# A fused attention, soft-MoE and maxout kernel: another order between its second and third stage, filler transposes, and one load taken a step earlier

## Chip, cores and metric

The kernel runs on one core of a Trainium2 chip. The metric is the device time of one execution in microseconds (us). The engines are TensorE (PE; its weight loads are PEld), VectorE (DVE), ScalarE (ACT), GpSimd (POOL) and SyncE (SP), which issues almost all DMAs of this kernel, in the order of its queue.

## What is computed

Three stages follow each other; everything is float32 to the outside, and the last stage's weights come in as float64.

```python
# 1. attention in chunks of 64 tokens: q, k, v are [8 batches, 8 heads, 576, 64]
scores = scale * q_c @ k_c.T;  attn = softmax(scores);  x = attn @ v_c
x = x as [4608 tokens, 512]
# 2. soft mixture of 8 experts, 4 slots each (32 slots)
logits = x @ phi                                   # [4608, 32]
d = softmax(logits over the tokens);  slot_input = d.T @ x      # [32, 512]
for e in range(8): slot_out[e] = relu(slot_input[e] @ w1[e]) @ w2[e]   # 512 -> 1024 -> 512
c = softmax(logits over the slots);  y = c @ slot_out
# 3. maxout
out = max(y @ w1, y @ w2, y @ w3) @ w_out          # 512 -> 768 -> 512
```

The softmax over the tokens is the reason for the narrow place that the change is about: no slot input exists before the last token's logits do.

## The kernel before, in words

**Items.** The first stage is cut into 36 items (`NI`): an item is 256 tokens of four heads. A hand-written list, `ORDER` (line 63), names the steps of one turn; the loop at line 573 runs the list once for every i, and a step with an offset works on another item than i (`item(f, d)` gives i + d). So in turn i, PE transposes q and k of item i + 3 (`Tq`, `Tk`, line 239), multiplies q and k of item i (`S`, line 271), transposes the scores (`PT`, line 303) and multiplies with v (`PV`, line 319) of item i - 1, and transposes x (`XT`, line 354) of item i - 2. ACT copies the transposed q and k out of PSUM (`qe`, `ke`, line 252) and takes the exponentials. Every fourth turn has the logits of 512 tokens (`lg`, line 372) and their part of the slot sum (`slp`, line 428).

**Weights of the third stage.** They arrive as float64 and are turned into float32 piece by piece, one of 30 pieces in each turn: `LR` (line 559) issues the load of raw piece i in turn i into a pool of two buffers (`r64_p`, line 151); in turn i + 1 ACT makes a first conversion (`da`, line 495), and DVE finishes it in three steps (`d0`, `d1`, `d2`, lines 500 to 506). `da` stands ahead of `ke` in ACT's queue.

**Loads.** SP issues, in each turn and in the order of the list, the raw piece, quarters of the first experts' weights (line 139), and q, k (line 179) and v (line 203) of later items. q and k of item i + 5 are loaded in turn i and transposed in turn i + 2. In turns 1 to 4 the last 64 tokens of all batches are loaded as well (line 191).

**Between items and experts** (lines 588 to 682). The last items run out; the logits of each group, kept in `lsb` as [slots, tokens], are transposed to [tokens, slots] (`emit_lt`, line 447: one PE transpose and one ACT copy a group; 9 groups). The last logits give the last maximum (`emit_final_max`), the exponentials, their transpose (`eps`, line 414), a maximum for all slots (`mt`, `mb`), the last slot product (`slp`), its accumulation on DVE (`acc`, line 437), the slot input (`sip`, line 669, copied to `siT`) and the sum of weights (`tot`, line 677). Then the first expert's product can start (`hps`, line 689).

**Experts** (line 778 on). Their weights, 32 pieces of 1 MB, go through a ring of 19 buffers; the buffers beyond twelve open when pools of the first stage close, and pieces 20 to 32 wait for buffers that the experts release. Then follow the last weights (`wr`) and the third stage, where PE computes all through (lines 872 and 909).

Of the kernel before, what the change touches and what calls it, by code (L numbers as in the profile page):

```python
# [8 lines left out]
F32 = mybir.dt.float32  # L9
# [11 lines left out]
def kernel(  # L21
# [14 lines left out]
    nc = tc.nc  # L36
    B, H, S, D = q.shape
    NT, DM = out.shape
    E, _, F = w1.shape
# [7 lines left out]
    NG = NU // 2  # L47
# [100 lines left out]
    v_p = tc.alloc_tile_pool(name="vp", bufs=1, side="right")  # L148
    q_p = tc.alloc_tile_pool(name="qp", bufs=3, side="right")
    raw_p = tc.alloc_tile_pool(name="raw", bufs=2, side="right")  # L150
    r64_p = tc.alloc_tile_pool(name="r64", bufs=2, side="right")
    ps_t = p1.enter_context(tc.tile_pool(name="ps_t", bufs=4, space=PSUM))
    ps_q = ps_t
    ps_s = p1.enter_context(tc.tile_pool(name="ps_s", bufs=1, space=PSUM))
# [18 lines left out]
    def load_T(j, nm):  # L173
        if J8 <= j < J8 + 4:
            return
        src = q if nm == "qr" else k
        t = raw_p.tile([128, 2, 4, D], F32, tag=nm, name=nm)
        h0 = 2 * (j % 4)
        nc.sync.dma_start(
            out=t, in_=src[DUS[j // 4], h0:h0 + 2, 0:2 * UNIT, :].rearrange("m (p r) d -> p m r d", r=4)  # L180
        )
        raw[nm, j] = t
# [195 lines left out]
    def emit_lcopy(g):  # L378
        nc.vector.tensor_copy(out=lsb[:, g, :], in_=lgs.pop(g))
# [32 lines left out]
    def emit_eT(g):  # L412
        ps = ps_t.tile([128, 128], F32, tag="t", name="eps")
        nc.tensor.transpose(ps, e_sb[g], ident)
        eps[g] = ps
# [18 lines left out]
    def emit_slot_acc(g):  # L434
        ps, nm = slp.pop(g), al.pop(g)
        if g:
            nc.vector.scalar_tensor_tensor(
                out=acc, in0=acc, scalar=nm[:, 1:2], in1=ps, op0=ALU.mult, op1=ALU.add
            )
        else:  # L440
            nc.vector.tensor_copy(out=acc, in_=ps)
# [2 lines left out]
        emit_slot_mm(g)  # L444
        emit_slot_acc(g)

    def emit_lt(g):
        ps = ps_q.tile([128, 128], F32, tag="t", name="lt")
        nc.tensor.transpose(ps, lsb[:, g, :], ident)
        nc.scalar.copy(out=lsb[:, g, :], in_=ps)  # L450

# [36 lines left out]
    def load_raw(n):  # L488
        src, dst = dec[n]
        t = r64_p.tile([128, DW, 2], I32, tag="r64", name="r64")[:, 0:dst.shape[-1], :]  # L490
        nc.sync.dma_start(out=t, in_=src.bitcast(I32).rearrange("p (n t) -> p n t", t=2))
        dec_t[n] = t
# [19 lines left out]
    if True:  # L512
        make_identity(nc, ident)
        nc.vector.tensor_copy(out=identb, in_=ident)
        for j in range(2):
            load_T(j, "qr")
            load_T(j, "kr")
        load_v(0, nc.scalar)
        load_v(1, nc.scalar)
        for t in vt:  # L520
            nc.gpsimd.memset(t[:, :, 128:130], 1.0)
            nc.gpsimd.memset(t[:, :, 194:196], 1.0)
        load_raw(0)
        nc.sync.dma_start(out=phi_sb, in_=phi.rearrange("(k p) s -> p k s", p=128))
        for j in range(3):
            emit_T(j)
            if j < 2:
                emit_qevac(j)
                emit_kevac(j)
            load_T(j + 2, "qr")  # L530
            load_T(j + 2, "kr")
        nc.gpsimd.memset(ones1, 1.0)

        def at(i, d):
            g, r = divmod(i - d, 4)
            return g if r == 0 and 0 <= g < NG else None

        def item(f, d):
            return lambda i: f(i + d) if 0 <= i + d < NI else None

        def group(f, d):
            return lambda i: f(at(i, d)) if at(i, d) is not None else None

        def dstep(part):
            def f(i):
                n = i - 1
                if 0 <= n < len(dec):
                    if part < 0:
                        decode_a(dec_t[n], dec[n][1])
                    else:  # L550
                        decode_b(dec_t[n], dec[n][1], part)
            return f

        def lstep_c(i):
            if i > 4:
                load_quarter()

        STEPS = {
            "LR": lambda i: load_raw(i) if 0 < i < len(dec) else None,
            "LQ": item(lambda j: load_T(j, "qr"), 5), "LK": item(lambda j: load_T(j, "kr"), 5),  # L560
            "LV": item(load_v, 2), "LC": lstep_c, "LD": lambda i: lstep_c(i) if i % 2 else None,
            "LS": lambda i: load_S(i - 1) if 1 <= i <= 4 else None,
            "VS": item(emit_vswap, 0),
            "qe": item(emit_qevac, 2), "S": item(emit_S, 0), "PT": item(emit_PT, -1), "PTe": item(emit_PTe, -1),
            "da": dstep(-1), "ke": item(emit_kevac, 2), "ex": group(emit_exps, 7), "sm": group(emit_slot_mm, 9),
            "sa": group(emit_slot_acc, 9), "Tq": item(lambda i: emit_T(i, ("qr",)), 3), "mx": item(emit_max, 0),
            "sub": item(emit_sub, 0), "XT": item(emit_XT, -2), "XTe": item(emit_XTe, -2),
            "d0": dstep(0), "d1": dstep(1), "d2": dstep(2), "PV": item(emit_PV, -1), "rd": item(emit_rd, -1),
            "rec": item(emit_rec, -1), "nrm": item(emit_norm, -1), "eT": group(emit_eT, 8), "eTe": group(emit_eTe, 8),
            "Tk": item(lambda i: emit_T(i, ("kr",)), 3), "lg": group(emit_logits, 6), "lc": group(emit_lcopy, 6),  # L570
            "st": group(emit_stats, 6), "ss": group(emit_ssum, 7),
        }
        for i in range(NI):
            for name in ORDER.split():
                STEPS[name](i)
            if i == len(dec) + 1:
                r64_p.release()
                open_rings(1)
                nc.vector.tensor_reduce(
                    out=sel, in_=ident.rearrange("p (g s) -> p s g", g=4), axis=AX.X, op=ALU.max  # L580
                )
            if i == NI - 4:
                raw_p.release()
                open_rings(1)
        q_p.release()
        open_rings(1)

        last = NG - 1
        emit_PT(NI - 1)
        emit_PTe(NI - 1)  # L590
        emit_eT(last - 1)
        emit_eTe(last - 1)
        emit_XT(NI - 2)
        emit_XTe(NI - 2)
        emit_PV(NI - 1)
        v_p.release()
        w1_p.release()
        open_rings(2)
        emit_rd(NI - 1)
        emit_rec(NI - 1)  # L600
        emit_norm(NI - 1)
        emit_slot(last - 1)
        xb_p.release()
        open_rings(1)
        for g in range(4):
            emit_lt(g)
        emit_XT(NI - 1)
        emit_XTe(NI - 1)
        emit_logits(last)
        xt_p.release()  # L610
        open_rings(1)
        emit_lcopy(last)
        emit_final_max()
        emit_eT(last)
        emit_eTe(last)
        emit_max_bcast()
        for g in range(4, last):
            emit_lt(g)
        emit_slot_mm(last)
        nc.vector.tensor_scalar(out=dg, in0=sel, scalar1=wv[:, 0:1], scalar2=None, op0=ALU.mult)  # L620
        emit_ssum(last)
        nc.vector.tensor_tensor(out=wv[:, 1:2], in0=wv[:, 0:1], in1=ssum, op=ALU.mult)
        emit_slot_acc(last)

    p1.close()
    m_p = ctx.enter_context(tc.tile_pool(name="m_p", bufs=1, side="right", reuse_waits="tile"))
# [37 lines left out]
    if True:  # L664
        for t in hzb:
            nc.gpsimd.memset(t, 0.0)
        sip = ps2.tile([128, KM, NS], F32, tag="b", name="sip")
        for kk in range(KM):
            nc.tensor.matmul(
# [1 line left out]
            )  # L671
        siT = m_p.tile([128, KM, NS], F32, name="siT")
        nc.vector.tensor_copy(out=siT, in_=sip)
        for g in range(4):
            nc.vector.tensor_copy(out=same[:, g, :], in_=sel)
        tot = ps2.tile([128, 1], F32, tag="b", name="tot")
        nc.tensor.matmul(tot, lhsT=same.rearrange("p g s -> p (g s)"), rhs=wv[:, 1:2], start=True, stop=True)
        nc.vector.tensor_scalar(out=wv[:, 2:3], in0=tot, scalar1=EPS, scalar2=None, op0=ALU.add)
        nc.vector.reciprocal(out=wv[:, 2:3], in_=wv[:, 2:3])
        lt = ps2.tile([128, 128], F32, tag="b", name="lt")  # L680
        nc.tensor.transpose(lt, lsb[:, NG - 1, :], ident)
        nc.scalar.copy(out=lsb[:, NG - 1, :], in_=lt)

        def emit_w1(e):
            ps = ps2b.tile([128, 256], F32, tag="h", name="hps")
# [14 lines left out]
        def emit_ht(e, hs):  # L700
            pt = ps2.tile([128, 2, 4, NS], F32, tag="b", name="hpt")
            for b in range(2):
                nc.tensor.transpose(
                    pt[:, b].rearrange("p j s -> p (j s)"), hs[:, 128 * b:128 * b + 128], ident
                )
            hz = hzb[e % 2]
            if e >= 2:
                nc.vector.memset(hz[:, :, SPE * (e - 2):SPE * (e - 1)], 0.0)
            nc.vector.tensor_copy(
                out=hz[:, :, SPE * e:SPE * e + SPE].rearrange("p (j b) s -> p b j s", b=2),  # L710
                in_=pt[:, :, :, SPE * e:SPE * e + SPE],
            )
# [62 lines left out]
                    b = stacks.pop(0)  # L775
                    ready.append((b, emit_stack(b)))

        emit_ht(0, emit_w1(0))
        for e in range(E):
            if e == E - 2:  # L780
                emit_w2(e, 0)
# [281 lines left out]
```

## Time and profile before

| | us |
|---|---|
| median of 3 timed runs (lowest, highest) | 450.44 (447.75, 451.75) |
| the profiled execution's own time | 447.13 |
| its span, first to last instruction | 445.3 |
| PE busy | 405.9 (91%) |
| DVE, ACT, POOL busy | 260.4, 215.7, 157.3 |
| mean granted clock of PE, in shares of full speed | 0.973 |

The items take the span up to about 180 us, the stretch between items and experts goes to about 193.5 us, the experts end at about 236 us and the third stage fills the rest. The DMA engines' busy share is 0.8 and more until about 190 us, near zero for some us there, full again until about 238 us, and 0.2 or less in the third stage. In what follows, a clock of 1.00 is 2.4 GHz and one of 0.50 is 1.2 GHz, PE's two levels; a mean between them is a stretch that had both.

### The profile page before, as it was taken

What the parts mean: (1) busy time and instruction counts of PE and PEld (TensorE: products, weight loads), DVE (VectorE), ACT (ScalarE), POOL (GpSimd) and SP (SyncE); (2) the same over time, 40 slices, a digit from 0 to 9 for tenths busy, and PEclk for the clock granted to TensorE, in tenths of its full rate; (3) what the DMA queues carried; (4) which work ended last, traced back from release to release, by engine and by line L of the source; (5) the groups of instructions that cost most, each with busy time, mean ns of one, the idle gap of its engine ahead of it and who ended that gap; (6) DMA issues with size and microseconds to landing.
All of it is one profiled execution on the core that took longest, in us unless ns stands there. A gap on an engine that the chain in (4) does not pass through costs nothing.

```text
span 445.3 us, 13226 instructions
## 1 busy us (share of the span) xinstructions
PE 405.9 (91%) x5505; PEld 303.4 (68%) x5505; DVE 260.4 (58%) x581; ACT 215.7 (48%) x393; POOL 157.3 (35%) x261
## 2 busy tenths in 40 slices
PE   5888978999899898789989799999999999999996
PEld 4766666767677676343345677888888888888884
DVE  0748777889788677426357996444444444444320
ACT  5647667868687575400026564433333333333230
POOL 4135333545344353000003585424333344333320
PEclk9989999999999899869999699999999999999999
DMA  8898799999999969949994001112121111111111
GB/s 264 253 269 265 216 282 358 339 336 309 339 334 313 305 203 379 411 180 381 414 410 202 1 0 73 47 49 61 36 69 47 47 49 48 49 55 63 49 47 71
DMA packets 65275, 84.80 MB, mean 190 GB/s; under 512 B 4800, under 2 KB 42688, under 8 KB 65216
## 3 DMA queue, kind: packets, MB, share of 16 engines
q1 hardware_dynamic: 64160, 83.44, 54.9%
q8 instruction: 43, 0.70, 0.6%
q10 hardware_dynamic: 1056, 0.52, 0.4%
q14 instruction: 16, 0.13, 0.1%
HBM read 74.51 MB, written 9.44 MB: 189 GB/s over the span
## 4 chain that ended last, share of the span: by engine, by line
PE 72%; DMA 12%; DVE 7%; ACT 5%; issue 3%; SPq 0%; POOL 0%; ACTq 0%; DVEq 0%
PE ops L909 34%; DMA r<-in_moe_w_dram 9%; PE h L872 9%; PE pss L271 4%; PE pso L319 3%; PE pskr L239 3%; PE pst L354 3%; PE pst L303 3%; PE psqr L239 3%; PE hps L689 2%; PE so L720 2%; PE lg L372 2%; ACT kT L252 2%; DMA qr<-in_q_dram 2%; PE slp L428 1%
## 5 line engine op out<-in xcount | busy, mean ns | idle before, releaser
L909 PE MATMUL ops<-wo,hhi 128*128 128x512 f32 x432 | 137.1, 399 | 0.0
L888 POOL TENSOR_TENSOR hlo<-a,hhi 128x512 fp32r<-128x512 f32 (+1 forms) x60 | 72.5, 1212 | 108.7 <-ACT hhi L885 108.4
L909 PEld LDWEIGHTS ops<-wo,hhi 128*128 128x128 f32 x432 | 81.3, 190 | 18.5
L881 DVE TENSOR_TENSOR a<-h,a 128x512 f32<-128x512 f32 (+1 forms) x60 | 38.1, 636 | 84.2 <-ACT a L877 83.9
L909 PE MATMUL ops<-wo,hlo 128*128 128x512 f32 x216 | 86.0, 398 | 0.0
L877 ACT COPY a<-h 128x512 f32<-128x512 f32 (+1 forms) x60 | 32.7, 545 | 95.1 <-PE h L872 94.5
L207 POOL COPY vt<-vt 128x256 f32<-128x256 f32 x36 | 14.6, 404 | 94.9 <-DMA vt<-in_v_dram 77.9
L909 PEld LDWEIGHTS ops<-wo,hlo 128*128 128x128 f32 x216 | 41.0, 190 | 10.2
L252 ACT COPY qT<-psqr 128x1024 uint16<-128x1024 uint16 x36 | 36.7, 1019 | 14.3 <-PE pss L271 11.3
L882 DVE TENSOR_TENSOR a<-h,a 128x512 f32<-128x512 f32 (+1 forms) x60 | 38.3, 638 | 6.2
L885 ACT CAST hhi<-a 128x512 fp32r<-128x512 f32 (+1 forms) x60 | 34.6, 580 | 9.5 <-DVE a L882 9.3
L252 ACT COPY kT<-pskr 128x1024 uint16<-128x1024 uint16 x36 | 36.1, 1003 | 0.5 <-PE pskr L239 0.5
L872 PE MATMUL h<-cstt,ast 128*128 128x512 f32 (+1 forms) x120 | 32.7, 385 | 0.3 <-DVE a L882 0.3
L287 DVE TENSOR_REDUCE mx<-pss 128x8 f32<-128x512 f32 x36 | 24.6, 683 | 14.1 <-PE pss L271 14.1
L209 POOL COPY vt<-vt 32x256 f32<-32x256 f32 x72 | 29.9, 415 | 4.3
L210 POOL COPY vt<-vt 32x256 f32<-32x256 f32 x72 | 29.2, 406 | 4.4
L319 PE MATMUL pso<-vt,pT 64*64 64x66 f32 x1152 | 26.8, 227 | 3.8 <-issue 3.3
L271 PE MATMUL pss<-kT,qT 64*64 64x64 f32 x1152 | 26.9, 230 | 3.5 <-ACT kT L252 1.6
L239 PE MATMUL pskr<-identb,kr 128*64 128x128 bf16 x512 | 23.0, 236 | 6.9 <-ACT kT L252 4.9
L319 PEld LDWEIGHTS pso<-vt,pT 64*64 64x64 f32 x1152 | 21.3, 136 | 10.6 <-issue 9.5
L854 POOL TENSOR_TENSOR wo<-tmp,wo 128x512 fp32r<-128x512 f32 x6 | 9.8, 1646 | 52.0 <-ACT wo L851 51.9
L239 PE MATMUL psqr<-identb,qr 128*64 128x128 bf16 x512 | 22.1, 232 | 5.9 <-DMA qr<-in_q_dram 4.9
(136 smaller groups left out, 588.4 us busy)
## 6 DMA issues: line engine op xcount, KB each, us to landing
w<-in_moe_w_dram SPq DMA_DIRECT2D x20, 1024.0 KB, 9.3
w<-in_moe_w_dram SPq DMA_DIRECT2D x44, 256.0 KB, 5.3
qr<-in_q_dram SPq DMA_DIRECT2D x32, 256.0 KB, 5.4
kr<-in_k_dram SPq DMA_DIRECT2D x32, 256.0 KB, 4.6
out_dram<-ob SPq DMA_DIRECT2D x32, 256.0 KB, 2.0
vt<-in_v_dram SPq DMA_DIRECT2D x30, 256.0 KB, 5.2
r<-in_moe_w_dram SPq DMA_DIRECT2D x18, 256.0 KB, 5.0
r<-in_moe_w_dram SPq DMA_DIRECT2D x12, 384.0 KB, 5.8
```

Of the source, the lines that this page charges most:

```text
L209: nc.gpsimd.tensor_copy(out=t[p:p + 32, :, 130:194], in_=t[p + 32:p + 64, :, 64:128])
L239: nc.tensor.transpose(dst, src[:, e, r, h, :], identb, tile_position=(0, 64 * e))
L252: copier(eng, j)(out=o, in_=x)
L271: nc.tensor.matmul(ps[64 * cp:64 * cp + 64, e, 128 * a + 64 * c2:128 * a + 64 * c2 + 64], lhsT=qT[j0 + a][64 * e:64 * e + 64, c0:c0 + CH], ...
L319: nc.tensor.matmul(ps[64 * cp:64 * cp + 64, c2, 66 * h:66 * h + 66], lhsT=t[64 * c2:64 * c2 + 64, h, 64 * cp:64 * cp + 64], rhs=vt[i % NV] ...
L872: nc.tensor.matmul(p, lhsT=a_st[t][:, i, f0:f0 + 128], rhs=cst(t0, n), start=True, stop=True)
L877: nc.scalar.copy(out=h_a[b, f], in_=h_ps[b, f][0])
L881: nc.vector.tensor_tensor(out=a, in0=ps[1], in1=a, op=ALU.max)
L882: nc.vector.tensor_tensor(out=a, in0=ps[2], in1=a, op=ALU.max)
L885: nc.scalar.copy(out=h_t[b][0][:, f, :], in_=h_a[b, f])
L888: nc.gpsimd.tensor_tensor(out=h_t[b][1][:, f, :], in0=h_a.pop((b, f)), in1=h_t[b][0][:, f, :].bitcast(F32), op=ALU.subtract)
L909: nc.tensor.matmul(ps, lhsT=a[:, f, 128 * t:128 * t + 128], rhs=wo_h[f // 2][:, f % 2, w, :], start=(f == 0 and n == 0), stop=(f == FB - 1 ...
```

## The change

There are three edits. The pool of raw pieces has three buffers in place of two, and turn i loads piece i + 1 in place of piece i; piece 1 is loaded ahead of the first turn. Between items and experts, the transposes of the logits are spread over other places, two of the nine go behind the first expert's product, the copies into `same` stand ahead of `sip`, and 14 transposes of the identity are added, which write a PSUM tile that nobody reads (`warm`). Nothing else differs.

```diff
--- before.py
+++ after.py
@@ -148,7 +148,7 @@
     v_p = tc.alloc_tile_pool(name="vp", bufs=1, side="right")
     q_p = tc.alloc_tile_pool(name="qp", bufs=3, side="right")
     raw_p = tc.alloc_tile_pool(name="raw", bufs=2, side="right")
-    r64_p = tc.alloc_tile_pool(name="r64", bufs=2, side="right")
+    r64_p = tc.alloc_tile_pool(name="r64", bufs=3, side="right")
     ps_t = p1.enter_context(tc.tile_pool(name="ps_t", bufs=4, space=PSUM))
     ps_q = ps_t
     ps_s = p1.enter_context(tc.tile_pool(name="ps_s", bufs=1, space=PSUM))
@@ -444,8 +444,8 @@
         emit_slot_mm(g)
         emit_slot_acc(g)
 
-    def emit_lt(g):
-        ps = ps_q.tile([128, 128], F32, tag="t", name="lt")
+    def emit_lt(g, pool=None, tag="t"):
+        ps = (pool or ps_t).tile([128, 128], F32, tag=tag, name="lt")
         nc.tensor.transpose(ps, lsb[:, g, :], ident)
         nc.scalar.copy(out=lsb[:, g, :], in_=ps)
 
@@ -529,6 +529,7 @@
                 emit_kevac(j)
             load_T(j + 2, "qr")
             load_T(j + 2, "kr")
+        load_raw(1)
         nc.gpsimd.memset(ones1, 1.0)
 
         def at(i, d):
@@ -556,7 +557,7 @@
                 load_quarter()
 
         STEPS = {
-            "LR": lambda i: load_raw(i) if 0 < i < len(dec) else None,
+            "LR": lambda i: load_raw(i + 1) if 0 < i < len(dec) - 1 else None,
             "LQ": item(lambda j: load_T(j, "qr"), 5), "LK": item(lambda j: load_T(j, "kr"), 5),
             "LV": item(load_v, 2), "LC": lstep_c, "LD": lambda i: lstep_c(i) if i % 2 else None,
             "LS": lambda i: load_S(i - 1) if 1 <= i <= 4 else None,
@@ -585,6 +586,12 @@
         q_p.release()
         open_rings(1)
 
+        warm = ps_s.tile([128, 512], F32, tag="s", name="warm")
+
+        def keep_busy(n):
+            for _ in range(n):
+                nc.tensor.transpose(warm[:, 0:128], ident, ident)
+
         last = NG - 1
         emit_PT(NI - 1)
         emit_PTe(NI - 1)
@@ -602,25 +609,32 @@
         emit_slot(last - 1)
         xb_p.release()
         open_rings(1)
-        for g in range(4):
-            emit_lt(g)
+        emit_lt(0)
+        emit_lt(1)
         emit_XT(NI - 1)
         emit_XTe(NI - 1)
         emit_logits(last)
         xt_p.release()
         open_rings(1)
         emit_lcopy(last)
+        emit_lt(2)
+        emit_lt(3)
+        keep_busy(5)
         emit_final_max()
+        emit_lt(4)
+        keep_busy(2)
         emit_eT(last)
         emit_eTe(last)
         emit_max_bcast()
-        for g in range(4, last):
-            emit_lt(g)
+        keep_busy(3)
         emit_slot_mm(last)
         nc.vector.tensor_scalar(out=dg, in0=sel, scalar1=wv[:, 0:1], scalar2=None, op0=ALU.mult)
         emit_ssum(last)
         nc.vector.tensor_tensor(out=wv[:, 1:2], in0=wv[:, 0:1], in1=ssum, op=ALU.mult)
         emit_slot_acc(last)
+        emit_lt(5)
+        emit_lt(6)
+        keep_busy(4)
 
     p1.close()
     m_p = ctx.enter_context(tc.tile_pool(name="m_p", bufs=1, side="right", reuse_waits="tile"))
@@ -664,6 +678,8 @@
     if True:
         for t in hzb:
             nc.gpsimd.memset(t, 0.0)
+        for g in range(4):
+            nc.vector.tensor_copy(out=same[:, g, :], in_=sel)
         sip = ps2.tile([128, KM, NS], F32, tag="b", name="sip")
         for kk in range(KM):
             nc.tensor.matmul(
@@ -671,15 +687,10 @@
             )
         siT = m_p.tile([128, KM, NS], F32, name="siT")
         nc.vector.tensor_copy(out=siT, in_=sip)
-        for g in range(4):
-            nc.vector.tensor_copy(out=same[:, g, :], in_=sel)
         tot = ps2.tile([128, 1], F32, tag="b", name="tot")
         nc.tensor.matmul(tot, lhsT=same.rearrange("p g s -> p (g s)"), rhs=wv[:, 1:2], start=True, stop=True)
         nc.vector.tensor_scalar(out=wv[:, 2:3], in0=tot, scalar1=EPS, scalar2=None, op0=ALU.add)
         nc.vector.reciprocal(out=wv[:, 2:3], in_=wv[:, 2:3])
-        lt = ps2.tile([128, 128], F32, tag="b", name="lt")
-        nc.tensor.transpose(lt, lsb[:, NG - 1, :], ident)
-        nc.scalar.copy(out=lsb[:, NG - 1, :], in_=lt)
 
         def emit_w1(e):
             ps = ps2b.tile([128, 256], F32, tag="h", name="hps")
@@ -775,7 +786,10 @@
                     b = stacks.pop(0)
                     ready.append((b, emit_stack(b)))
 
-        emit_ht(0, emit_w1(0))
+        hs = emit_w1(0)
+        emit_lt(NG - 2, ps2, "b")
+        emit_lt(NG - 1, ps2, "b")
+        emit_ht(0, hs)
         for e in range(E):
             if e == E - 2:
                 emit_w2(e, 0)
```


How the instructions stand now, at three places. On SP, at the end of the prologue and in the first two turns (`r` are the raw pieces, `qr` and `kr` q and k, `qrs` and `krs` their last tokens, `vt` is v), before:

```order
L179 DMA qr<-in_q_dram 128x2x256
L179 DMA kr<-in_k_dram 128x2x256
L179 DMA qr<-in_q_dram 128x2x256
L203 DMA vt_116<-in_v_dram 128x4x128
L179 DMA kr<-in_k_dram 128x2x256
L491 DMA r_335<-in_moe_w_dram 128x512
L179 DMA qr<-in_q_dram 128x2x256
L191 DMA qrs<-in_q_dram 128x1x256 x2
```


and with the change:

```order
L179 DMA qr<-in_q_dram 128x2x256
L179 DMA kr<-in_k_dram 128x2x256
L491 DMA r_265<-in_moe_w_dram 128x512
L179 DMA qr<-in_q_dram 128x2x256
L203 DMA vt_116<-in_v_dram 128x4x128
L179 DMA kr<-in_k_dram 128x2x256
L491 DMA r_337<-in_moe_w_dram 128x512
L179 DMA qr<-in_q_dram 128x2x256
```


One load of a raw piece is now ahead of the first turn, and each later one is a piece further at the same place of its turn.

On PE, from the last but one slot product to the last one (`lt` transposes logits, `pst` x, `lg` are logits, `mt` and `mb` the maxima, `eps` the exponentials), before:

```order
L428 MATMUL slp<-x,e 32x512 x4
L449 MATMUL lt<-ident,lsb 128x128 x4
L354 MATMUL pst<-ident,x 128x128 x4
L372 MATMUL lg<-xT,phi_sb 32x128 x16
L464 MATMUL mt<-ident,nm 1x128
L414 MATMUL eps<-ident,et 128x128
L476 MATMUL mb<-ones_67,phi_sb 128x1
L449 MATMUL lt<-ident,lsb 128x128 x4
L428 MATMUL slp<-x,e 32x512 x4
```


and with the change, from the row behind that first slot product on:

```order
L449 MATMUL lt<-ident,lsb 128x128 x2
L354 MATMUL pst<-ident,x 128x128 x4
L372 MATMUL lg<-xT,phi_sb 32x128 x16
L449 MATMUL lt<-ident,lsb 128x128 x2
L593 MATMUL warm<-ident 128x128 x5
L464 MATMUL mt<-ident,nm 1x128
L449 MATMUL lt<-ident,lsb 128x128
L593 MATMUL warm<-ident 128x128 x2
L414 MATMUL eps<-ident,et 128x128
L476 MATMUL mb<-ones_67,phi_sb 128x1
L593 MATMUL warm<-ident 128x128 x3
L428 MATMUL slp<-x,e 32x512 x4
```


Two of the four `lt` ahead of `pst` have gone behind the logits, all of the next four have left the place ahead of `slp`, and ten fillers stand in that piece.

On PE, from the last slot product to the first expert's second product, before:

```order
L428 MATMUL slp<-x,e 32x512 x4
L669 MATMUL sip<-dg,acc 128x32 x4
L677 MATMUL tot<-wv,same 128x1
L681 MATMUL lt<-ident,lsb 128x128
L689 MATMUL hps<-w,siT 32x256 x16
L703 MATMUL hpt<-ident,hs 128x128 x2
```


and with the change:

```order
L428 MATMUL slp<-x,e 32x512 x4
L449 MATMUL lt<-ident,lsb 128x128 x2
L593 MATMUL warm<-ident 128x128 x4
L685 MATMUL sip<-dg,acc 128x32 x4
L691 MATMUL tot<-wv,same 128x1
L700 MATMUL hps<-w,siT 32x256 x16
L449 MATMUL lt<-ident,lsb 128x128 x2
L714 MATMUL hpt<-ident,hs 128x128 x2
```


Two `lt` and four fillers now lie between `slp` and `sip`, and the `lt` that stood ahead of `hps` is behind it with another one.

## Rows read from the trace of the kernel before

**Rows 1.** Stretches: busy of each engine (count), granted clock, DMA share, GB/s.

```profile
20.00:60.00 40.00, 33.03 (x870) 25.67 (x867) 28.00 (x70) 26.40 (x42) 14.13 (x36) 0.96 0.86 253
60.00:140.00 80.00, 72.44 (x1956) 55.69 (x1958) 67.23 (x175) 60.16 (x106) 36.85 (x90) 1.00 1.00 332
140.00:180.00 40.00, 35.79 (x919) 27.16 (x921) 29.69 (x74) 25.27 (x45) 16.48 (x40) 0.96 0.90 298
```

**Rows 2.** Waits of ScalarE, whole span (releaser: us, times, longest).

```profile
ACT wm L495 <- DMA r<-in_moe_w_dram: 17.4, 12, 3.0
```

**Rows 3.** Waits of ScalarE between 20 and 60 us.

```profile
ACT wm L495 <- DMA r<-in_moe_w_dram: 9.3, 4, 3.0
```

**Rows 4.** Chain of waits, in order of time: start us, us, what.

```profile
20.40 6.06 DMA r<-in_moe_w_dram
...
26.48 0.43 ACT wm L495
...
28.33 0.59 PE pst L303 x4
```

**Rows 5.** DMA issues of the page: queue, count, KB each, us to landing.

```profile
qr<-in_q_dram SPq DMA_DIRECT2D x32, 256.0 KB, 5.4
...
r<-in_moe_w_dram SPq DMA_DIRECT2D x18, 256.0 KB, 5.0
r<-in_moe_w_dram SPq DMA_DIRECT2D x12, 384.0 KB, 5.8
```

**Rows 6.** Issues of line 179 from 60 to 140 us: ns min/median/max, first and last start.

```profile
L179 SPq DMA_DIRECT2D kr<-in_k_dram x18: 367/384/949, 61.6 to 137.5; - x18
```

**Rows 7.** Chain of waits between items and experts.

```profile
180.23 1.00 PE slp L428 x8
...
185.11 0.50 ACT et L461 x2
...
186.29 0.94 PE lt L449 x4
187.23 1.91 PE slp L428 x8
189.16 0.76 DVE acc L437
...
190.06 1.90 PE sip L669 x8
...
191.98 0.29 DVE siT L673
192.27 0.35 DVE same L675 x4
...
192.67 0.59 PE tot L677 x2
...
193.57 3.48 PE hps L689 x32
...
198.05 1.86 PE hps L689 x32
```

**Rows 8.** Three stretches, as in the first group.

```profile
86.50:97.50 11.00, 10.70 (x277) 7.88 (x272) 9.68 (x24) 8.94 (x16) 5.67 (x14) 1.00 1.00 327
184.00:186.40 2.40, 1.01 (x6) 0.69 (x6) 1.54 (x8) 0.85 (x4) 0.00 (x0) 1.00 1.04 418
191.00:196.50 5.50, 4.78 (x38) 2.80 (x39) 0.96 (x7) 0.27 (x1) 0.00 (x0) 0.50 0.07 26
```

**Rows 9.** The first of these for line 239, the bf16 transposes.

```profile
86.50:97.50 11.00, 3.31 (x86) 2.40 (x80) 1.00 1.00 327
```

**Rows 10.** The first of these for line 303, the f32 transposes of the scores.

```profile
86.50:97.50 11.00, 1.96 (x12) 1.25 (x12) 1.00 1.00 327
```

**Rows 11.** The first of these for line 354, the f32 transposes of x.

```profile
86.50:97.50 11.00, 1.80 (x10) 1.15 (x11) 1.00 1.00 327
```

**Rows 12.** PE idle before work on expert weights that ended on their DMA: us, times.

```profile
  DMA w<-in_moe_w_dram: 0.3, 1
```

## The prediction, made before the changed kernel ran

> **What bounds the kernel now.** I read the stretches first, by engine, clock and DMA share, then the waits of ACT, then the chain of waits through the narrow place behind the items, and last the clock there.
>
> Among the items, three stretches differ [rows 1]. From 60 to 140 us the DMA engines are full (share 1.00, 332 GB/s) and PE is busy for 72.44 of 80 us; nothing that only asks earlier for the same bytes can gain much there. From 20 to 60 us neither is full: PE is busy for 33.03 of 40 us at a mean clock of 0.96, and the DMA share is 0.86. From 140 to 180 us PE has 35.79 of 40.
>
> What PE lacks from 20 to 60 us is seen on ACT. Its first conversion of a raw weight piece waits for that piece's DMA, 12 times and 17.4 us in all [rows 2], of which 4 times and 9.3 us lie between 20 and 60 us [rows 3]. The chain shows one case: the load issued at 20.40 takes 6.06 us, and only then ACT converts, at 26.48 [rows 4]; the copy of k that PE's next scores need stands behind it in ACT's queue. The page gives 5.0 and 5.8 us as the median from issue to landing of the raw pieces [rows 5]. The items' length can be had from the loads of k, one an item: 18 issues from 61.6 to 137.5 us, so 75.9 / 17 = 4.5 us [rows 6]. A piece is issued one item before its use, so its landing is longer than its lead.
>
> Behind the items the reader is to follow one chain, from the last but one slot product at 180.23 to the first expert's product, which starts at 193.57 and takes 3.48 us, where the next one takes 1.86 [rows 7]. From 184.0 to 186.4 us PE was busy for 1.01 of 2.40 us at clock 1.00, and from 191 to 196.5 us it is granted 0.50, that is 1.2 GHz, while the DMA engines move 26 GB/s, since the expert weights wait for buffers that this product has to release [rows 8]. In the experts, PE's idle time that ended on their weights is 0.3 us [rows 12], so what is gained ahead of them is passed on, and the third stage follows them unchanged.
>
> **The raw pieces.** A piece gets a lead of two items, some 9 us, against 5.0 to 5.8 us of landing, so nearly all 17.4 us of ACT's waits should go. What comes back is less. From 20 to 60 us the bounds are the 9.3 us of waits, PE's missing 40 - 33.03 = 7.0 us, and the idle time of the DMA engines, 40 x (1 - 0.86) = 5.6 us, because the same bytes must still arrive. The smallest counts; I take 5.0, since full DMA engines without any gap would be needed for all of it. What is late next there are q, k and v themselves. From 60 to 140 us I take nothing, for the DMA engines are full; from 140 to 180 us nothing, PE being the fuller one. Upper end: 5.6, and half of the 8.1 us of waits outside that stretch, about 9. Lower end: nothing comes back, and the piece that now goes out ahead of the first turn pushes q, k and v back by 256 KB at 253 GB/s, 1.0 us; so -1. On SP the extra issue has no wait of its own, as it has a fresh buffer; the later ones wait for the same release as before (three buffers, one piece further), so nothing is queued longer behind them. **-5.0 us.**
>
> **The narrow place.** Price of one transpose: 4 take 0.59 us at full clock [rows 4], 0.15 each; at 186.29 four take 0.94, 0.24 each, as the clock falls. Step by step against [rows 7]:
> - Two of the four transposes ahead of the last transposes of x leave: 2 x 0.15 = 0.3, and their ACT copies no longer hold a PSUM buffer. -0.4.
> - Behind the logits stand two `lt`, five fillers, one `lt`, two fillers, 10 x 0.15 = 1.5 us, in a gap that PE has anyway between 184.0 and the exponentials' end at 185.61 (0.5 us from 185.11). The max transposes in their midst may start 0.2 us later, but its result is needed only for `sip`, over 2 us further on. +0.1.
> - The four transposes ahead of the last slot product (0.94) become three fillers (0.45). -0.5.
> - The slot product at full clock, as at 180.23: 1.91 becomes 1.00. -0.9.
> - Two `lt` and four fillers, 0.9 us, lie beside the accumulation, which keeps `sip` back by 190.06 - 189.14 = 0.92 us anyway. 0. If DVE's step were not there they would cost 0.9.
> - `sip`, 1.90 us at half clock. At full clock no row has it; it lies between 0.95 (half) and 1.90 (weight loads unchanged). The other two products here halve, so I take 1.0. -0.9.
> - `same`, `tot` and `lt` kept the expert's product from 192.27 to 193.57, 1.3 us. The copies now run under `sip`, `tot` beside the 0.29 us of `siT`, `lt` behind the product. -1.2.
> - The first expert's product at full clock: 3.48 becomes 1.86. -1.6.
>
> Sum **-5.4 us**, with ends at -1 (clock as before, fillers on the path) and -6.5. The DMA engines can pass it on: they stand nearly still for the 5.5 us from 191 [rows 8].
>
> **Does the clock stay up?** It does if transposes count as work of PE. From 86.5 to 97.5 us PE was busy for 10.70 us, and lines 239, 303 and 354, transposes all, had 3.31 + 1.96 + 1.80 = 7.07 of these, at clock 1.00 throughout [rows 8 to 11]. It fell behind a stretch in which PE mostly stood still, 1.01 of 2.40 us [rows 8]. With the fillers, PE has work there almost without a break. The Trainium skill, "TensorE: Matmul & The Clock Gate", section "Part 4: PE-mode transpose", says that transposes do not count as busy PE for the clock gate. By that rule the fillers would be no help and the clock would fall as before; the row, with two thirds transposes at 2.4 GHz, speaks against it, though no row shows transposes alone.
>
> **Sum.** -5.0 - 5.4 = -10.4. The profiled execution took 447.13 us (span 445.3) and would take 436.7. It lies 3.3 us under the median of the three timed runs, so I forecast from that median: 450.44 - 10.4 = **440.0 us**. I count 1% (4.5 us) as the least change that a measurement of this kernel can tell, so faster means under 445.9, slower over 454.9.
>
> **Rivals.**
> 1. *The clock falls all the same* (transposes do not hold it). For it: no row shows transposes alone, and each filler is one. Against: the clock of 1.00 with two thirds transposes [rows 8 to 11]. Then the two halved products and `sip` stay slow, the 10 transposes take 0.24 each and overrun their gap by some 0.8, the six beside the accumulation by 0.5, and 0.4 + 0.5 + 1.2 of the order's gain remains less those: about -1 for the narrow place, -6 in all: 444.4 us. Chance 0.12.
> 2. *The raw wait only hid the DMA's.* If q, k or v are late as soon as the raw pieces are not, the items gain nothing, as from 60 to 140 us. For it: share 0.86 is not far from full, and the loads of 20 to 60 us have the smallest rate. Against: 5.6 us of idle DMA time. Only the narrow place pays: 450.44 - 5.4 = 445.0. Chance 0.17.
> 3. *Both*: the change does not do what it says; -1: 449.4. Chance 0.07.
> 4. *Slower: raw pieces overtake q and k.* In the full stretch each item's q and k, with a lead of two items (9 us) and a landing of 5.4 [rows 5], would share the DMA engines with one piece more in flight. A piece is 256 or 384 KB, 0.8 to 1.2 us at 332 GB/s. If PE waited 0.9 us for q in each of the 17 items from 60 to 140 us, that is 15.3 us; with the narrow place's 5.4 and 5.0 from before 60 us the time would be 455.3. It decides where the landing of q grows from 5.4 to over 9 us; it has 3.6 us to spare, and the bytes an item stay the same, which speaks against it. Chance 0.05.
>
> The forecast has 0.59, with its own range of 436 to 444 us. The range takes in rivals 1 and 2 and the upper ends of both terms (9 and 6.5, from 450.44: 434.9), and stops short of rival 3: 435 to 447 us. Faster: 0.58 of the forecast's 0.59, most of rival 1 (0.08) and half of rival 2 (0.08), so 0.74; slower: 0.04 of rival 4's 0.05; the same: the other 0.22.
>
> **What will show it.** In the changed profile: ACT's waits for raw pieces from 17.4 to under 3 us; PE's busy share from 20 to 60 us up, DMA share there over 0.93; no stretch of 0.50 between the last logits and the second expert; the first expert's product in about 1.9 us, and 3.4 us in place of 193.57 - 187.23 = 6.3 us from the start of the last slot product to the start of that one; the DMA engines without a hole there. Wrong would be: the raw waits gone and PE waiting for q, k or v instead; PE waiting for expert weights for more than the 0.3 us; or a low clock in the narrow place with the fillers running through it.

## The result, and the profile after

The change makes the kernel faster by half of what was forecast. The changed kernel takes 444.85 us (median of 20 runs, 440.29 to 450.66), the kernel before, run beside it, 451.81 us (20 runs, 445.4 to 457.86). The ratio is 0.9879 with a 95% interval of 0.984 to 0.9918, or -5.5 us (-7.2 to -3.7); it leaves out, of either kernel, the runs more than 1.5% above its fastest, and so lies nearer to 1 than the ratio of the two medians, which are 7.0 us apart. Forecast were 440.0 us and -10.4. A second set of runs of the changed kernel (f4 below) gives 0.9868 (0.9831 to 0.9906).

The profiled execution took 440.29 us, its span is 438.5 us. Its narrow place is as forecast. First the chain of waits, which answers to [rows 7]: start, duration, what.

```profile
178.15 1.00 PE slp L428 x8
...
183.75 0.48 PE warm L593 x3
184.22 1.04 PE slp L428 x8
...
185.29 0.76 DVE acc L437
...
186.09 1.09 PE sip L685 x8
...
187.21 0.30 DVE siT L689
...
187.55 1.93 PE hps L700 x32
```

From one slot product to the first expert's product are 187.55 - 178.15 = 9.40 us, where [rows 7] have 193.57 - 180.23 = 13.34, and that product takes 1.93 us where it took 3.48. Together -5.5 us, against -5.4 in the sum. The stretches, with the columns of [rows 1], show the clock and the DMA engines there and what became of the items:

```profile
20.00:60.00 40.00, 33.10 (x930) 25.82 (x933) 30.20 (x76) 28.09 (x44) 16.40 (x37) 1.00 0.91 258
60.00:140.00 80.00, 72.06 (x1905) 55.08 (x1894) 66.62 (x169) 58.04 (x102) 38.21 (x90) 0.98 0.99 328
140.00:178.00 38.00, 34.54 (x922) 26.16 (x921) 29.67 (x75) 26.08 (x47) 16.56 (x40) 1.00 0.94 317
178.00:188.00 10.00, 9.57 (x107) 5.88 (x100) 5.48 (x23) 3.24 (x14) 0.56 (x2) 1.00 1.04 411
188.00:190.00 2.00, 1.86 (x30) 0.85 (x22) 0.44 (x1) 0.22 (x2) 0.00 (x0) 1.00 0.75 194
190.00:192.00 2.00, 1.81 (x30) 1.14 (x34) 0.23 (x2) 0.22 (x2) 0.00 (x0) 1.00 0.66 231
```

From 178 to 188 us PE is busy for 9.57 of 10 us at 1.00, and the DMA engines move 411 GB/s. The place where [rows 8] have 26 GB/s for 5.5 us now lies in the last two rows: a dip to 194 and 231 GB/s is left of the hole. In the first row PE's busy time has hardly moved (33.03 to 33.10 of 40), and the DMA share has gone from 0.86 to 0.91 only, not over 0.93. Busy time hides some progress there, as the same work takes longer at the lower clock (`slp` 1.91 us against 1.00 in [rows 7]): in these 40 us the trace has 930 matmuls at 1.00 where it had 870 at 0.96. ACT waits for no raw piece any more: the 17.4 us of [rows 2] have no row left, and with them went PE's waits for ACT's copies of k. What took their place stands in the waits of PE on the loads of q and k (us, times, longest). Before:

```profile
PE psqr L239 <- DMA qr<-in_q_dram: 4.9, 3, 3.8
PE pskr L239 <- ACT kT L252: 4.9, 6, 1.8
...
PE pss L271 <- ACT kT L252: 1.6, 3, 0.7
...
PE pskr L239 <- DMA kr<-in_k_dram: 0.4, 1, 0.4
```

and after, where no row with `kT` is left:

```profile
PE psqr L239 <- DMA qr<-in_q_dram: 7.7, 7, 4.1
...
PE pskr L239 <- DMA kr<-in_k_dram: 2.9, 4, 1.3
```

The items got to the last but one slot product 180.23 - 178.15 = 2.1 us sooner, where 5.0 were forecast. So this one pair of profiles tells of -2.1 - 5.5, less some 0.8 given back in experts and third stage: 445.3 - 438.5 = 6.8 us. What the experiments had to find was why the raw loads pay so little, and whether the 5.5 us of the narrow place are there in every execution.

### The profile page after: what moved, and what is told of

Same layout as the page of the kernel before. It is cut to its first block, busy times and chain, and to the rows that moved or that the text cites. A ratio compares the mean times of both kernels' runs of the same rounds, so it can differ in the third digit from the quotient of the medians.

```text
span 438.5 us, 13254 instructions
## 1 busy us (share of the span) xinstructions
PE 402.1 (92%) x5519; PEld 301.1 (69%) x5519; DVE 262.6 (60%) x581; ACT 216.0 (49%) x393; POOL 159.7 (36%) x261
## 4 chain that ended last, share of the span: by engine, by line
PE 73%; DVE 9%; DMA 9%; issue 4%; ACT 3%; POOL 0%; SPq 0%; DVEq 0%; ACTq 0%; POOLq 0%
PE ops L923 33%; PE h L886 7%; DMA qr<-in_q_dram 4%; PE pso L319 4%; PE pskr L239 4%; PE pss L271 4%; DMA kr<-in_k_dram 4%; PE psqr L239 4%; PE pst L354 4%; PE pst L303 3%; PE lg L372 2%; PE hps L700 2%; PE so L731 2%; PE slp L428 2%; DVE tmp L506 1%
## 5 line engine op out<-in xcount | busy, mean ns | idle before, releaser
L207 POOL COPY vt<-vt 128x256 f32<-128x256 f32 x36 | 16.4, 456 | 89.7 <-DMA vt<-in_v_dram 74.4
L923 PEld LDWEIGHTS ops<-wo,hlo 128*128 128x128 f32 x216 | 41.0, 190 | 10.1
L239 PE MATMUL psqr<-identb,qr 128*64 128x128 bf16 x512 | 23.0, 236 | 13.2 <-DMA qr<-in_q_dram 7.7
L209 POOL COPY vt<-vt 32x256 f32<-32x256 f32 x72 | 30.6, 425 | 4.3
L210 POOL COPY vt<-vt 32x256 f32<-32x256 f32 x72 | 30.0, 416 | 4.4
L239 PEld LDWEIGHTS <-qr 128*64 128x64 bf16 x512 | 17.1, 118 | 19.4 <-DMA qr<-in_q_dram 10.8
L308 ACT ACTIVATE pT<-pst 128x512 f32<-128x512 f32 x36 | 21.5, 596 | 16.6 <-PE pst L303 16.4
L359 ACT COPY xT<-pst 128x512 f32<-128x512 f32 x36 | 21.4, 593 | 16.8 <-PE lg L372 10.2
```

The source lines that it names most:

```text
L209: nc.gpsimd.tensor_copy(out=t[p:p + 32, :, 130:194], in_=t[p + 32:p + 64, :, 64:128])
L239: nc.tensor.transpose(dst, src[:, e, r, h, :], identb, tile_position=(0, 64 * e))
L923: nc.tensor.matmul(ps, lhsT=a[:, f, 128 * t:128 * t + 128], rhs=wo_h[f // 2][:, f % 2, w, :], start=(f == 0 and n == 0), stop=(f == FB - 1 ...
```

## The experiments

Runs made together share their runs of the kernel before: e1 to e4, e5 to e8, f1 to f4, g1 to g4.

| run | median us (runs) | ratio to before, 95% interval |
|---|---|---|
| e1, narrow place alone | 449.03 (12) | 0.9931, 0.9878 to 0.9984 |
| e2, raw loads alone | 448.20 (12) | 0.9906, 0.9856 to 0.9956 |
| e3, no fillers | 446.37 (6) | none given |
| e4, fillers alone | 447.87 (12) | 0.9941, 0.9902 to 0.998 |
| e5, half the raw bytes | 439.43 (4) | 0.9791, 0.9716 to 0.9866 |
| e8, half the bytes, old lead | 438.67 (4) | 0.9721, 0.9634 to 0.9807 |
| e6, q and k further ahead | 443.11 (4) | 0.9827, 0.9743 to 0.991 |
| e7, 65 fillers | 451.88 (1) | one run |
| f3, no fillers, again | 445.46 (6) | 0.9885, 0.984 to 0.9931 |
| f4, the change, again | 444.10 (6) | 0.9868, 0.9831 to 0.9906 |
| g1, q and k further ahead, no fillers | 445.85 (12) | 0.9911, 0.9877 to 0.9944 |
| g2, ring of 11 alone | 445.03 (6) | 0.9899, 0.9858 to 0.9941 |

### Each part alone (e1, e2)

e1 is the changed kernel with the raw loads of before; e2 is the kernel before with this edit:

```diff
-    r64_p = tc.alloc_tile_pool(name="r64", bufs=2, side="right")
+    r64_p = tc.alloc_tile_pool(name="r64", bufs=3, side="right")
...
+        load_raw(1)
...
-            "LR": lambda i: load_raw(i) if 0 < i < len(dec) else None,
+            "LR": lambda i: load_raw(i + 1) if 0 < i < len(dec) - 1 else None,
```

> The narrow place alone, raw loads as before. Theory (the narrow place is worth what was forecast, the raw loads little): 5.5 us faster than before, the last slot product to the first expert's product 3.4 us, ACT's waits for raw pieces 17 us as before. Rival (the raw loads carry a good part): 5.5 us too by its own account, but then well behind the whole change; a third of it if the clock in the narrow place holds only because the items run tighter.

> Three buffers and the earlier raw load alone. Theory (the DMA engines bound the items, so q and k come late where the raw pieces no longer do): 2 us faster than before, ACT's waits for raw pieces under 1 us, PE's waits for q and k about 10 us in place of 5. Rival (the term of 5 us was right and one profiled execution hides it): 5 us faster, PE's waits for q and k as before.

The narrow place alone gives -3.1 us (-5.5 to -0.7 of 452.4), the raw loads alone -4.3 (-6.5 to -2.0). The two add up to -7.4; the whole change gives -5.5 to -6.0, within the intervals. Neither theory is borne out cleanly: the raw loads bring more than the 2 us of the first, and the narrow place less than its 5.5. The intervals are wide: each still holds what was forecast for its part, so these two runs alone do not say which part fell short by more. Yet the profile of e1 has the changed narrow place as it should be, 196.54 - 187.11 = 9.43 us. So the kernel before was profiled again, to see whether its narrow place is often shorter than 13.3 us. In e2 the raw waits are gone and PE's waits for q and k read as the first theory has them:

```profile
PE psqr L239 <- DMA qr<-in_q_dram: 9.4, 7, 4.3
PE pskr L239 <- DMA kr<-in_k_dram: 2.7, 4, 1.6
```

### The kernel before, profiled again (f1, f2, g3, g4)

No edit; one execution each.

> The kernel before, unchanged, profiled once more. Theory (its narrow place is not always as slow as in the first profile, so the change saves less on the average than the 5.5 us seen there): from the start of the last slot product but one to the start of the first expert's product 11 to 12.5 us in place of 13.3, the first product 1.9 us in at least one of two looks. Rival (it is always that slow): 13.3 and 3.5 us again.

> The second look at the kernel before; the two theories expect what they expect of the first.

> The kernel before, a third further look. Theory (in some executions the clock falls in its narrow place and in some not): either 13.3 us from the last slot product but one to the first expert's product with a product of 3.5 us, or 11.05 us with one of 1.9. Rival (the first profile was an exception): 11.05 and 1.9 here and in the next look.

> The kernel before, a fourth further look; the two theories expect what they expect of the third.

The chain of waits of f1:

```profile
182.21 1.00 PE slp L428 x8
...
188.96 1.06 PE slp L428 x8
...
190.94 1.06 PE sip L669 x8
...
193.26 1.91 PE hps L689 x32
```

and of g3:

```profile
189.48 1.00 PE slp L428 x8
...
196.22 1.83 PE slp L428 x8
...
198.98 1.90 PE sip L669 x8
...
202.49 3.62 PE hps L689 x32
```

and of g4:

```profile
187.25 1.00 PE slp L428 x8
...
198.30 3.12 PE hps L689 x32
```

The same two rows of f2, and then of e2:

```profile
183.21 0.99 PE slp L428 x8
...
194.26 1.91 PE hps L689 x32
```

```profile
184.03 1.00 PE slp L428 x8
...
197.16 3.62 PE hps L690 x32
```

In f1, as in f2, the clock never fell in this place: 193.26 - 182.21 = 11.05 us, and a product of 1.91. In g3 it fell as in [rows 7]: 13.01 us and 3.62. In g4 it fell late: 11.05 us again, but a product of 3.12. The executions took 445.13 us (f1), 446.16 (f2), 456.51 (g3) and 452.28 (g4); the two without the fall are the shorter ones, though the ends of their items differ too. With the first profile and that of e2 (13.13 us and 3.62), there are six profiles of one and the same narrow place of the kernel before, from the slot product's start to the end of the first expert's product: 16.8, 16.8, 13.0, 13.0, 16.6 and 14.2 us, a mean of 15.05. The changed one takes 9.40 + 1.93 = 11.3 in the first profile and the same within 0.1 in e1, f4 and g2. So the change saves up to 5.5 us where the clock had fallen and 1.6 where it had not, 3.7 in the mean of these few profiles; e1's timed runs say 3.1.

### Fillers (e3, f3, e4, e7, f4)

e3 and f3 drop the tile `warm` and leave `keep_busy` empty; e7 has one number changed; e4 is the kernel before with fillers at three places of its old order.

```diff
-        keep_busy(5)
+        keep_busy(65)
```

> The whole change without the 14 fillers. Theory (the fillers hold the clock): the clock falls to 0.50 within the narrow place, the first expert's product takes 3.5 us or the last slot product 1.9, and the time is 3 us above that of the whole change, 3 to 4 us under before. Rival (the new order alone keeps PE busy enough): clock 1.00 there, time as the whole change.

> The kernel before with 16 fillers in the narrow place (7 behind the last logits, 3 behind the max transposes, 6 behind the last slot product) and its old order. Theory (transposes hold the clock): clock 1.00 through the narrow place, slot product 1.0, first expert's product 1.9 us, 2.5 to 3.3 us faster than before. Rival (transposes do not count for the clock): 0.50 there as before and 1 us slower by the fillers.

> The whole change with 65 fillers in place of 5 behind the last logits: some 10 us in which PE runs transposes and nothing else. Theory (transposes hold the clock): clock 1.00 through them, 0.15 us each, the time 8 to 9 us above that of the whole change. Rival (they do not count): the clock falls to 0.50 within them, 0.24 us each, and stays low until the expert's products, 14 us or more above.

> The whole change without fillers, again, with more rounds. Theory (the new order alone keeps PE busy enough, as the first look showed): narrow place at clock 1.00, time within 1.5 us of the whole change in this call. Rival (the first look was luck): clock 0.50 in the narrow place, 3 us slower than the whole change.

> The whole change, unchanged, beside the run without fillers. Both theories: narrow place as in its first profile (9.4 us from the last slot product but one to the first expert's product), some 7 us under before; the items end somewhere between 178 and 184 us, as DMA landings differ from one execution to the next.

Without fillers, the chain of e3 reads:

```profile
180.71 1.00 PE slp L428 x8
...
186.36 1.11 PE slp L428 x8
...
188.30 1.09 PE sip L682 x8
...
189.78 1.91 PE hps L697 x32
```

9.07 us, 0.33 less than with them, and every product at full clock; f3 and g1 have 9.06 and 9.07. With the new order alone the clock stayed up in all three profiles. That rivals the theory that the fillers hold it, and timed side by side f3 and f4 are alike (0.9885 and 0.9868). Over all profiles, the clock fell in the narrow place in none of eleven with the new order, eight with fillers and three without, and in five of seven with the old one, e4 with its fillers among them. Three profiles can't exclude that the fillers save a rare fall.

In e4, the old order with fillers, the clock stayed up through the slot product (1.06) and `sip` (1.06), but behind `siT`, where DVE still makes `same` and no filler stands, it fell:

```profile
190.60:193.80 3.20, 2.23 (x21) 1.93 (x17) 1.38 (x6) 0.00 (x0) 0.56 (x2) 1.00 0.98 385
193.80:197.20 3.40, 3.40 (x34) 1.44 (x33) 0.32 (x2) 0.27 (x1) 0.00 (x0) 0.50 0.12 43
```

Its product took 3.43 us, so half of the theory's case came. It is one profile, and the kernel before holds the clock at times without any filler. In the timed runs e4 is 2.7 us (0.9 to 4.4) faster than the kernel before, so in the old order the fillers do pay on the whole; how, one profile does not show.

That transposes can hold the clock is shown by e7: 65 of them in a row, and the stretch that they fill.

```profile
187.67 7.10 PE warm L593 x65
```

```profile
187.70:194.70 7.00, 7.00 (x66) 6.97 (x65) 0.64 (x4) 0.92 (x5) 0.00 (x0) 1.00 0.97 351
```

PE did nothing but transposes for 7 us, the granted clock is 1.00 (2.4 GHz), and what follows ran at full speed; the run took 7 to 8 us more than the change's medians. The Trainium skill, "TensorE: Matmul & The Clock Gate", section "Part 4: PE-mode transpose", says that they do not count as busy PE in the same way and that the full clock does not engage for them; here the measurement decides against it, at least for a clock that is up already and for 7 us. One back-to-back transpose costs 7.10 / 65 = 0.11 us, not the 0.15 that I had from groups of four.

### Why the items gain so little (e5, e8, e6, g1, g2)

e5 loads half of every raw piece and uses it for both halves of the piece's columns, so the second half of the weights repeats the first (`n2` is half of a piece's columns); e8 does the same with the old lead of one item.

```diff
-        nc.sync.dma_start(out=t, in_=src.bitcast(I32).rearrange("p (n t) -> p n t", t=2))
...
+        nc.sync.dma_start(out=t, in_=src[:, 0:n2].bitcast(I32).rearrange("p (n t) -> p n t", t=2))
+        t = t.unsqueeze(1).to_broadcast([128, 2, n2, 2])
```

> The whole change with half the bytes of every raw piece: the second half of a piece's columns repeats the first, with the same number of elements on ACT and DVE. 4.7 MB less over the items, 14 us of the DMA engines at 332 GB/s. Theory (the rate of the DMA engines bounds the items once the raw waits are gone): PE's waits for q and k shrink from 10 us to the 5 us of the start, DMA share from 60 to 140 us under 0.95, 5 to 10 us faster than the whole change. Rival (the items are bound by PE and the issue order, the q and k waits are of no weight): within 2 us of the whole change.

> The same half bytes, but two buffers and the raw load one item ahead as before; narrow place changed. Theory (rate): most of what half the bytes bring comes here too, as pieces half as large land sooner: ACT's raw waits from 17 us to under 6, within 3 us of the run with half bytes and the longer lead. Rival (the lead counts by itself): the raw waits stay over 10 us and the time is 4 us or more behind that run.

By their ratios e5 is 0.9879 - 0.9791 = 0.0088, some 4.0 us, under the changed kernel, and e8 0.0158, some 7.1 us. They have four runs each, and e5's interval overlaps that of the change. In e5 the DMA share from 60 to 140 us is 0.94, in e8 0.92, where the change has 0.99 (0.95 in f4), and in e5 the pieces of q land in 4.8 us in place of 5.4:

```profile
qr<-in_q_dram SPq DMA_DIRECT2D x32, 256.0 KB, 4.8
```

e8 is as fast although ACT waits for raw pieces nearly as before:

```profile
ACT wm L499 <- DMA r<-in_moe_w_dram: 13.6, 10, 2.4
```

So the expectation for its waits (under 6 us) was wrong, and that is the telling part: 13.6 us of waiting on ACT cost nothing against e5 that four runs of each can tell, while 4.7 MB less did pay, with either lead. The items answer to bytes, as the theory of full DMA engines has it. Against it stands that PE's waits for q and k did not shrink in e5 (6.8 and 3.5 us), and that 4 to 7 us came back of the 14 that these bytes take at 332 GB/s.

PE's waits show what the earlier load exchanges. There are seven profiles with whole pieces and the old lead, and six with whole pieces, the new lead and a ring of 12. From the one to the other, PE's waits for ACT's copies of q and k go from 6.9 us in the mean (4.2 to 10.2) to 0.2, its waits for the loads of q and k rise from 7.1 (5.3 to 10.1) to 10.1 (7.8 to 12.1), and those put down to nothing that the trace shows ("issue"), among the items, from 10.2 to 12.6. The last but one slot product starts at 184.6 us in the mean with the old lead (180.2 to 189.5) and at 182.5 with the new one (178.2 to 184.8): 2.1 us again, with a scatter that is larger.

e6 takes the next wait away, that for q and k: three buffers in their pool, loads six items ahead, and a ring of 11 buffers to make room. g1 is the same without fillers, g2 the smaller ring alone.

```diff
-    NRING = 12
+    NRING = 11
...
-    raw_p = tc.alloc_tile_pool(name="raw", bufs=2, side="right")
+    raw_p = tc.alloc_tile_pool(name="raw", bufs=3, side="right")
...
+            if j == 2:
+                load_T(5, "qr")
+                load_T(5, "kr")
...
-            "LQ": item(lambda j: load_T(j, "qr"), 5), "LK": item(lambda j: load_T(j, "kr"), 5),
+            "LQ": item(lambda j: load_T(j, "qr"), 6), "LK": item(lambda j: load_T(j, "kr"), 6),
```

> The whole change with q and k loaded one item further ahead (three buffers in place of two; to make room, the ring has 11 buffers in place of 12, so one more MB of expert weights is left for the experts' time, 2.5 us of the DMA engines there). Theory (rate): the waits for q and k stay near 10 us or turn into waits for raw pieces or v, and the last slot product but one is not reached more than 1 us sooner. Rival (their lead is too short): PE's waits for q and k fall to the 5 us of the start and the items end 3 us or more sooner.

> The whole change with q and k loaded one item further ahead (ring of 11) and without the fillers. Theory (the short lead of q and k is what took the raw waits' place): PE's waits for q and k at the 5 us of the start, the last slot product but one before 178 us, 3 us under the run with a ring of 11 alone; narrow place 9.1 us at clock 1.00. Rival (the DMA engines' rate): the same within 1 us as the ring of 11 alone.

> The whole change with a ring of 11 buffers in place of 12 and nothing else: the control for the two runs with q and k further ahead. One MB of expert weights moves from the items to the experts. Theory: the same as the whole change within 2 us, PE's waits for q and k near 10 us. Rival (it is the smaller load in the items that made the other run fast): as fast as that run, 1.5 us or more under the whole change.

e6's four runs looked better than the change (0.9827), but no gain is shown: its control g2 has 0.9899 with an interval that overlaps, and g1, with more runs, 0.9911. PE's waits for q and k fall to those of the start, and "issue" waits come up. The waits of PE in g1:

```profile
PE pss L271 <- issue: 6.0, 4, 2.8
PE pso L319 <- issue: 5.5, 7, 2.4
PE psqr L239 <- DMA qr<-in_q_dram: 5.3, 3, 4.2
```

Its stretches:

```profile
20.00:60.00 40.00, 35.49 (x987) 27.55 (x987) 32.14 (x80) 28.87 (x46) 18.30 (x41) 1.00 0.97 272
60.00:140.00 80.00, 68.40 (x1772) 52.13 (x1776) 60.95 (x154) 55.34 (x95) 36.86 (x85) 0.98 0.96 311
```

From 20 to 60 us PE runs 987 matmuls in place of 930 and is busy for 35.49 us in place of 33.10, with the DMA share at 0.97: there the longer lead does what the raw one was to do. From 60 to 140 us PE is busy for 3.7 us less than in the first profile of the change, but f4, the same change, has 69.50 us there, so part of that is scatter. What those "issue" waits are was not found. No kernel that computes the whole result was measured faster than the changed one beyond the intervals.

## Why the prediction was wrong, point by point

Both terms of the sum were too large; the directions and the mechanism of each held.

- **The raw pieces, -5.0: one step that failed.** ACT's waits are gone, and of the smallest bound, 5.6 us of idle DMA engines, the share's rise from 0.86 to 0.91 used 40 x 0.05 = 2.0. The step that failed is taking 5.0 of these 5.6, as if nothing else would hold PE back once the raw pieces were there. In the first pair PE waited 10.6 us for the loads of q and k in place of 5.3 while its waits for ACT's copies of k went; over all profiles 6.7 us of such waits went and 5.4 came back, 3.0 on q and k and 2.4 as "issue". Only fewer bytes (e5, e8) made the items clearly shorter. What limits them beyond that stays open, as the "issue" waits were not explained. Measured: -4.3 (-6.5 to -2.0) alone, 2.1 us in the pair of profiles, and 0.9879 / 0.9931 = 0.995, some -2.4 us, on top of the narrow place. That q and k would be late next was named, and named as a sign of being wrong, and is what the waits show; in the sum it had no price beyond the 0.6 us between 5.6 and 5.0.
- **The narrow place, -5.4: the other step that failed.** Its order terms and its clock terms agree with the profile to 0.1 us in the sum (`sip` 1.09 for 1.0, the product 1.93 for 1.86, the distance of the two starts 187.55 - 184.22 = 3.33 for 3.4). What failed is that the three terms "at full clock", 0.9, 0.9 and 1.6, were priced as if every execution lost them. Six profiles show the clock down there through the place in three, late in one and not at all in two. In the mean the place saves 3.7 us, in timed runs 3.1 (0.7 to 5.5). That the first pair of profiles agrees with the 5.4 confirms the size of the terms, not how often they are paid: the sum was read from the very profile, with the clock down, that it is compared with.
- **The clock stays up.** Right, in all eleven profiles of the changed order; and right that transposes can hold it (e7). But the fillers are not the reason that can be shown: the order alone did it in three profiles.
- **The DMA engines pass it on; the experts don't wait.** Right in the main: 411 GB/s up to the expert's product and a dip to 194 in place of the hole, and PE's idle time on expert weights is 0.3 us as before.
- **The base.** The forecast stood on a median of three runs, 450.44; twenty gave 451.81. This did no harm to the difference, but the spread from 445.4 to 457.86 shows that one profile is one draw.
- **Rivals.** Rival 2 (q and k late) is what happened in part; rivals 1 (the clock falls all the same), 3 (both) and 4 (slower) did not happen. The landing of q that rival 4 turns on stayed at 5.4 us.

In sum, -3.1 to -3.7 for the narrow place and -2.4 to -4.3 for the raw loads stand where -5.4 and -5.0 were. How the 5 us that are missing divide between the two the runs do not tell any closer.

## What to carry to other kernels

Where a term rests on a low clock, one profile says what it costs when it happens, not how often: look at the same place in several executions and weight the price. A wait on one load that is cured by loading it earlier can come back as waits on the next load: here that left 2 to 4 us of a bound of 5.6. Price the load that is late next, too. Order the work around a narrow place so that the engine stands idle less, before filling the holes with work that nobody needs.

## What was not expected of the hardware

- PE transposes of 128x128 f32, alone for 7 us, kept the granted clock at 1.00, at 0.11 us each (e7).
- The same instructions, with no edit, ran the narrow place in 13.0 to 13.3 us up to the expert's product or in 11.05, by whether the clock had fallen there; the timed runs of the kernel before spread over 12 us.
- 13.6 us of waiting on ACT for raw pieces (e8) cost nothing that four runs can tell against none of it (e5), while half the bytes of those pieces saved 4 to 7 us.
